# Two of eight token pairs read in a turned layout and normalised there, with nine warming products instead of fifteen

## The chip, the cores and the metric

The kernel runs on one core of a Trainium2 chip. The metric is the device time of one execution in microseconds. The engines are TensorE (PE, the matrix engine, with its weight loads shown as PEld), VectorE (DVE), ScalarE (ACT), GpSimd (POOL) and SyncE (SP, which here issues nearly all DMAs). All data are float32.

## What is computed

```python
def reference(x, wqkv, w_phi, wo, w1, b1, w2):      # x: 2048 x 512
    xn = layernorm(x)                                # no scale, no shift, eps 1e-5
    q, k, v = heads(xn @ wqkv)                       # 32 heads of 16
    phi = lambda p: concat(softmax(p), softmax(-p))
    phi_q, phi_k = phi(q @ w_phi), phi(k @ w_phi)    # w_phi: 16 x 16 for each head
    kv, z = phi_k.T @ v, phi_k.sum(tokens)           # over all 2048 tokens
    s = (phi_q @ kv / (phi_q @ z + 1e-6)) @ wo
    g = silu(mish(xn @ w1 + b1) @ w2)                # 512 -> 1792 -> 512
    return x + s * g
```

## The kernel before

The 2048 tokens are 16 tiles of 128, and two neighbouring tiles form a pair c (0 to 7; tiles 2c and 2c+1). Every matrix operand is kept as a high part (rounded to the matrix engine's fp32r format) and a low part, the rest, and each product is made of three: low by high, high by low, high by high. On top of that the products go by a scheme of Strassen's kind with seven products of blocks in place of eight. Each pair needs for it seven blocks of its normalised, turned x, `xc[c][0]` to `xc[c][6]`: three are x's own quarters, four are sums and differences of them (`xs`). For pairs 0 to 3 these blocks are parts of the tiles `fh`, `fl` (seven of each), which the feed-forward part reads directly; for pairs 4 to 7 they lie in one tile `xc<c>`, and two DMAs copy them to a buffer `xd` in memory, from which later parts load them back.

`norm(t)` makes a tile: load x, statistics on DVE (`st`, `mv`), `rs` = 1/sqrt(var + eps) with a power on POOL, `nb` = -mean times rs, the normalisation of `x` on DVE or ACT, then four PE transposes (128x128 each, a product with the identity `ident`) into the PSUM bank `pt<t>`, from which ACT and DVE read the high and low parts and the differences. Ahead of everything PE multiplies a tile of ones with itself into `wake`, 15 times. `phit`, the 128x512 block matrix of w_phi, is `phic` (a DMA) times a mask; `fold` multiplies it into the weights of k and q on PE (`wkf`, `wqf`), so k and q come out with w_phi applied. `ws1` to `ws4` are sums of weight blocks for the seven products.

The order is written out by hand. ORDER lists the parts of the program (N4 is the normalisation of tile 4, Kc0 a product of pair 0 for k and v, Fa0 one of the first feed-forward matrix, P its weights' preparation, G the second feed-forward matrix, E the end). PLAN lists every recorded operation, as part.number, with a letter where an operation can go to more than one engine (V DVE, G POOL, A ACT); the instructions are issued in that order, so it is the order on each engine's queue. PLACE lists the buffer that each new tile takes. The first DMA of PLAN goes to ACT's queue, all others to SP's. Where a POOL operation stands within 24 places behind a DVE operation that shares a port with it, it waits for that one. Line 293 of the profile is the one line from which every recorded operation is issued (294 in the kernel after the change), so that operations are told apart by the names of their tiles: `kx`, `ky`, `kz`, `kj` products for k and v, `qx` to `qz` for q, `fx`, `fy`, `fz` for the first feed-forward matrix, `y` for the second, `kvp` the sum over tokens, `pn`, `pw` the attention's output; `k<t>p`, `k<t>m`, `k<t>e`, `k<t>s`, `k<t>r` the softmax of tile t; `ha`, `hb`, `hc` the feed-forward sums; `w1a`, `w1s` its weights, each with h and l for the two parts.

Of the kernel before, what the change touches and what calls it, by code (L numbers as in the profile page):

```python
# [16 lines left out]
P = 128  # L17
# [11 lines left out]
WAKE, EACH, NEAR = 15, 2, 24  # L29
# [12 lines left out]
N4.0 N1.0 @.0 @.15 @.1 N4.3 @.2 @.17 @.3 N0.0 @.4 wv0.0 @.5 @.18 @.6 @.7 N4.1 @.19 @.8 @.9 N1.1 wv1.0 @.10 @.16G @.11  # L42
@.20 @.12 N4.2 N1.2 @.13 wq1.0 N1.3 @.14 N4.4 N1.4 N2.0 kh.0 N4.5 N1.5 N4.6 N1.6V N0.1 N4.7 N1.7 kh.1 N4.8 N5.0 N0.2
N1.8 N4.9V wv0.1 N2.3 N6.0 N0.3 kh.2 N0.4 N4.10 N8.3 P4.0 kh.4 N0.5 N4.11 N0.6V N5.1A N6.3 N1.9 wv0.2G N0.7 N4.12 kh.5
kh.3 N5.2 kl.0 N0.8 kh.6 kh.7 wv1.1 N4.13 wq0.0 kl.4 N1.10 wv1.2G N0.9 kl.1 Ka2.0 N1.11 kd.0 N12.0 kl.2 N4.14 N8.0
N0.10 wq1.1 kl.3 N1.12A b1.0 P0.0 Ka2.1A N0.11 kd.1G Ka2.2 N5.3 N2.1 wq1.2A N5.4 N2.2 N2.4 kl.5 N5.5A Ka0.0 N1.13 N2.5
N1.14 N2.6 Ka2.3 N2.7 Ka0.1 N5.6 N1.15G N3.0 kl.6 N5.7 N3.1A N5.8G N1.16 Kc0.0 kl.7 N1.17 Ka0.2A N2.8 N1.18G N8.4
N2.9A wq1.3 k4.0G N1.19 N6.1 N6.4 N2.10 wq1.4A N3.2 N2.11 Kc0.1 N1.20 N2.12 N10.0 N3.3 N2.13 N1.21V k2.0 N3.4 ks.0G
wq0.1 N1.22 N8.1 N3.5A Kd0.0 N2.14 N5.9 wq0.2A Kc0.2A N5.10 N6.2 N3.6 wq0.3 N3.7 ks.1 Kd0.1 N6.5 k2.1V N3.8V N8.2 N8.5
wq0.4A N6.6 N8.6 P0.5 N3.9 wq1.5 N12.3 wq0.5 Kb0.0 Kc0.3 N8.7 N6.7 N3.10 Kd0.2A Kc0.4 N3.11G k4.1 Kb0.1 N5.11G N3.12  # L50
N9.0 N7.0 Kd0.3 N9.1A P0.6G Ka1.0 N8.8 Kc0.5V N5.12 N3.13 N7.1A Kc0.6V Kb2.0 N3.14G ks.2G P0.1G Kd0.4 Kd0.5V Kb0.2V
N6.8 N8.9A Ka1.1A Ka1.2 Kc0.7 N5.13 Kd0.6V N8.10 Kb1.0 N3.15 Ka1.3 N6.9A P0.2G Kc0.8 N5.14G N8.11 N8.12 Kd0.7 k4.2G
Kb1.2 N6.10 N1.23 Kb1.1V Kc0.9 N6.11 N9.2 N7.2 N7.3 N5.15 N5.16 N3.16 Kd0.8 Kc1.0 N9.3 Kb2.1A P0.3G N1.24G N6.12 Kb2.2
# [266 lines left out]
def block_kernel(ctx: ExitStack, tc: tile.TileContext, x, wqkT, wv, phi, wo, w1, b1, w2, out):  # L320
# [33 lines left out]
    def f32(t):  # L354
        return t.bitcast(F32)
# [43 lines left out]
    for _ in range(WAKE):  # L399
        PE.matmul(wake, ones, ones, start=True, stop=True)  # L400
# [704 lines left out]
```

## Time and profile before

| | |
|---|---|
| median of 3 runs | 485.85 us (485.78 to 486.92) |
| the profiled execution | 485.87 us |
| its span, first to last instruction | 484.2 us |
| PE busy | 478.1 us, 99% |
| DVE, ACT, POOL busy | 444.5, 286.7, 262.7 us |
| granted PE clock | full in all slices |

The span is what the rows of the profile cover; 1.7 us of the execution lie around it. Busy shares are averages: PE's matmuls overlap, each row's duration includes its pipeline, and the chain of waits shows what a group of them moves the end by. In rows of groups the columns are line, engine, operation, out<-in with the number of rows, then busy us and mean ns. A row of the waits names who waits, for whom, and the us in total, the number of times and the longest.

### The profile page before, as it was taken

To read this page: it belongs to the slowest core of one execution; us is meant where nothing else is said; L and a number is where in the kernel's file an instruction comes from. 1 tells how busy PE (TensorE), PEld (TensorE's weight loads), DVE (VectorE), ACT (ScalarE), POOL (GpSimd) and SP (SyncE) were. 2 spreads that over 40 slices of the span, in tenths; PEclk is the share of its full clock that TensorE was granted. 3 is DMA by queue.
4 is the path that set the end of the run, shared out by engine and by line. 5 is a ranking of instruction groups with operands and counts; after the bars stand their busy time and mean duration, and the time that the engine had idled before them with its cause. 6 is when DMAs were issued, how large, how long until landed. Compare 5 with 4: busy or idle time off the path is not lost.

```text
span 484.2 us, 10225 instructions
## 1 busy us (share of the span) xinstructions
PE 478.1 (99%) x3820; PEld 426.1 (88%) x3820; DVE 444.5 (92%) x874; ACT 286.7 (59%) x450; POOL 262.7 (54%) x219
## 2 busy tenths in 40 slices
PE   8999999999999999999999999999999999999996
PEld 7888888888888899889888778788999999999996
DVE  6999999899999989999999999989897899999985
ACT  4896645656446343453425745576868677699711
POOL 4988988885671275897888575350312231120042
PEclk9999999999999999999999999999999999999999
DMA  8921672779876889977875739633766346747354
GB/s 309 324 88 45 204 243 63 265 228 303 346 265 211 310 333 375 322 223 247 259 280 153 293 115 345 213 106 126 242 219 206 96 138 203 229 134 214 121 192 145
DMA packets 68642, 105.70 MB, mean 218 GB/s; under 512 B 6896, under 2 KB 37744, under 8 KB 68592
## 3 DMA queue, kind: packets, MB, share of 16 engines
q1 hardware_dynamic: 68448, 104.79, 64.5%
q8 instruction: 30, 0.49, 0.4%
q10 hardware_dynamic: 144, 0.26, 0.2%
q14 instruction: 20, 0.16, 0.1%
HBM read 60.60 MB, written 44.43 MB: 217 GB/s over the span
## 4 chain that ended last, share of the span: by engine, by line
PE 97%; DVE 1%; DMA 1%; POOL 0%; ACT 0%; issue 0%
PE y L293 29%; PE fx L293 16%; PE pw L293 9%; PE fy L293 8%; PE kx L293 8%; PE qx L293 5%; PE ky L293 4%; PE fz L293 4%; PE qy L293 2%; PE kj L293 2%; PE pn L293 2%; PE kz L293 2%; PE kvp L293 2%; PE pt L293 1%; PE qz L293 1%; PE wqf L293 1%
## 5 line engine op out<-in xcount | busy, mean ns | idle before, releaser
L293 POOL TENSOR_TENSOR r<-r 128x128 f32<-128x128 f32 (+1 forms) x40 | 24.5, 626 | 90.8 <-DVE al L293 30.5
L293 DVE TENSOR_TENSOR al<-r,ah 128x896 fp32r<-128x896 f32 x55 | 59.3, 1094 | 8.0 <-PE y L293 3.5
L293 ACT ACTIVATE ah<-r 128x896 fp32r<-128x896 f32 x56 | 52.4, 947 | 21.2 <-PE y L293 7.7
L293 PE MATMUL y<-w2h,al 128*128 128x256 f32 x160 | 45.4, 284 | 0.0
L293 PE MATMUL y<-w2h,ah 128*128 128x256 f32 x160 | 45.3, 283 | 0.0
L293 PE MATMUL y<-w2l,ah 128*128 128x256 f32 x160 | 45.3, 283 | 0.0
L293 PE MATMUL y<-w2t,ah 128*128 128x256 f32 x224 | 42.3, 283 | 0.0
L293 DVE TENSOR_TENSOR r<-r 128x128 f32<-128x128 f32 (+1 forms) x128 | 39.6, 354 | 1.3 <-POOL r L293 1.2
L293 ACT ACTIVATE r<-r 128x512 f32<-128x512 f32 x56 | 33.1, 621 | 10.3 <-DMA r<-hd 10.2
L293 PE MATMUL fx<-fh,w1b 128*128 128x512 f32 x112 | 38.5, 391 | 0.0
L293 PEld LDWEIGHTS y<-w2t,ah 128*128 128x128 f32 x224 | 34.9, 192 | 0.0
L293 PE MATMUL y<-w2t,al 128*128 128x256 f32 x112 | 31.7, 283 | 0.0
L293 PE MATMUL y<-w2g,ah 128*128 128x256 f32 x160 | 31.6, 283 | 0.0
L293 PEld LDWEIGHTS y<-w2h,al 128*128 128x128 f32 x160 | 30.7, 192 | 0.4 <-ACT w2m L293 0.4
L293 PEld LDWEIGHTS y<-w2l,ah 128*128 128x128 f32 x160 | 30.7, 192 | 0.0
L293 PEld LDWEIGHTS y<-w2h,ah 128*128 128x128 f32 x160 | 30.7, 192 | 0.0
L293 PEld LDWEIGHTS fx<-fh,w1b 128*128 128x128 f32 x112 | 21.1, 188 | 4.6 <-issue 0.4
L293 PEld LDWEIGHTS y<-w2g,ah 128*128 128x128 f32 x160 | 24.9, 192 | 0.1
L293 PE MATMUL y<-w2g,al 128*128 128x256 f32 x80 | 22.6, 283 | 0.0
L293 PE MATMUL fx<-fl,w1b 128*128 128x512 f32 x56 | 21.9, 391 | 0.0
L293 PEld LDWEIGHTS y<-w2t,al 128*128 128x128 f32 x112 | 21.5, 192 | 0.0
L293 POOL TENSOR_TENSOR sr<-yy,sr 128x512 f32<-128x512 f32 x3 | 3.8, 1293 | 29.3 <-DVE al L293 25.9
(769 smaller groups left out, 1719.4 us busy)
## 6 DMA issues: line engine op xcount, KB each, us to landing
r<-hd SPq DMA_DIRECT2D x56, 256.0 KB, 3.6
xd<-xc SPq DMA_DIRECT2D x8, 896.0 KB, 5.7
w1b<-w1d SPq DMA_DIRECT2D x14, 512.0 KB, 5.6
w1b<-w1d SPq DMA_DIRECT2D x14, 384.0 KB, 5.8
so<-so SPq DMA_DIRECT2D x16, 256.0 KB, 3.4
x<-x SPq DMA_DIRECT2D x15, 256.0 KB, 4.8
w1a<-w SPq DMA_DIRECT2D x7, 512.0 KB, 4.5
w1d<-w1sh SPq DMA_DIRECT2D x7, 512.0 KB, 2.9
```

Of the source, the lines that this page charges most:

```text
L293: ins = getattr(e, m)(*a, **k)
```

## The change

- A new array xT holds pairs 6 and 7 of x turned ahead of time: for each pair four 128x256 blocks, 512 KB in all, with the features on the partitions and the tokens along the row. Tiles 12 to 15 are made by the new `turned(c)`. x itself is still loaded, token by row, for the statistics, which ACT makes with accumulating passes; mean and factor are turned by a small DMA to memory (`md`) and spread over the partitions by another (`mb`); `xt`, the load of xT, is then shifted and scaled along its rows by two 128x1024 operations. The blocks are split and subtracted from `xt` in SBUF; there are no transposes, no `pt`, no `nb` and no `xr` for these tiles.
- WAKE is 9 instead of 15, and the warming products are one entry of PLAN.
- PLAN and PLACE are new as a whole; ORDER is as it was. `phic` is the first DMA (on ACT's queue), and `phit` is made on DVE; it was POOL's.

```diff
-WAKE, EACH, NEAR = 15, 2, 24
+TURNED = (6, 7)
+WAKE, EACH, NEAR = 9, 2, 24
...
-N4.0 N1.0 @.0 @.15 @.1 N4.3 @.2 @.17 @.3 N0.0 @.4 wv0.0 @.5 @.18 @.6 @.7 N4.1 @.19 @.8 @.9 N1.1 wv1.0 @.10 @.16G @.11
+@.1 @.0 N4.3 @.2V N4.4 N4.0 @.5 kl.0 N1.0 N4.1 @.3 N4.2 N0.0 wv0.0 @.4 wq1.0 N4.5 wv1.0 N4.6 N4.7 N1.1 N5.0 N4.8 N1.2
...
     wake = bank([P, P], "wake")
-    for _ in range(WAKE):
-        PE.matmul(wake, ones, ones, start=True, stop=True)
+    with one():
+        for _ in range(WAKE):
+            PE.matmul(wake, ones, ones, start=True, stop=True)
...
+    def turned(c):
+        mv = alloc("st", [P, 2, 2], f"mv{c}")
+        for i in range(2):
+            xx, junk = load_x(2 * c + i), s2(f"junk{c}{i}")
+            A.activation(junk, xx, AF.Copy, scale=-1.0 / D, accum_out=mv[:, i, 0:1])
+            A.activation(junk, xx, AF.Square, bias=mv[:, i, 0:1], accum_out=mv[:, i, 1:2])
+        V.tensor_scalar(mv[:, :, 1], mv[:, :, 1], 1.0 / D, 1e-5, op0=ALU.mult, op1=ALU.add)
+        G.tensor_tensor(mv[:, :, 1], mv[:, :, 1], mhalf, op=ALU.pow)
+        md = dram.tile([4, P], F32, name=f"md{c}")
+        Q.dma_start(md.rearrange("a p -> p a"), mv.rearrange("p t m -> p (t m)"))
+        mb = s2(f"mb{c}")
+        Q.dma_start(mb, md.rearrange("a p -> (a p)")[None, :].to_broadcast([P, D]))
+        xt, d = slot([P, 4, 2, P], f"xt{c}"), slot([P, 4, 2, P], f"xs{c}")
+        Q.dma_start(xt.rearrange("p b k n -> p (b k n)"), xT[TURNED.index(c)].rearrange("p b k n -> p (b k n)"))
+        u = xt.rearrange("p (t b) k n -> p t (b k) n", t=2)
+        m = mb.rearrange("p (t m n) -> p t m n", t=2, m=2)
+        for i, op in ((0, ALU.add), (1, ALU.mult)):
+            either(u, u, m[:, :, i, None, :].to_broadcast([P, 2, 4, P]), op=op)
...
+            w = alloc("tq", [P, 2, 7, 2, P], f"xc{c}", F32R)
...
+            xc[c] = [(w[:, 0, x], w[:, 1, x]) for x in range(7)]
+            split(xt[:, 0:3], w[:, 0, 0:3], w[:, 1, 0:3], either)
+        for i, a, b in ((0, xt[:, 3], xt[:, 0]), (1, xt[:, 2], d[:, 0]), (2, xt[:, 2], xt[:, 3]), (3, xt[:, 1], d[:, 1])):
+            either(d[:, i], a, b, op=ALU.subtract)
...
+        split(d, w[:, 0, 3:], w[:, 1, 3:], either)
+        for u in range(2):
+            Q.dma_start(xd[:, u, :, :, c % 4, :].rearrange("p c k n -> p (c k) n"), f32(w)[:, u].rearrange("p c k n -> p (c k) n"))
+
     def norm(t):
+        if t // 2 in TURNED:
+            if t % 2 == 0:
+                turned(t // 2)
+            return
```

The start of PE's queue before, up to the first block product:

```order
L293 MATMUL wake_99<-ones_84 128x128 x15
L293 MATMUL wkf01_147<-phit_101,wkT00_137 128x128 x4
L293 MATMUL pt1_173<-ident_83,x1_170 128x128 x4
L293 MATMUL pt4_156<-ident_83,x4_151 128x128 x4
L293 MATMUL wkf11_148<-phit_101,wkT01_138 128x128 x4
L293 MATMUL pt0_167<-ident_83,x0_164 128x128 x4
L293 MATMUL pt5_184<-ident_83,x5_153 128x128 x4
L293 MATMUL wkf21_181<-phit_101,wkT10_139 128x128 x4
L293 MATMUL wkf31_182<-phit_101,wkT11_140 128x128 x4
L293 MATMUL kx2_187<-wv0h_142,fl00_104 128x512
```

The same place after the change:

```order
L294 MATMUL wake_99<-ones_84 128x128 x9
L294 MATMUL wkf21_181<-phit_101,wkT10_139 128x128 x4
L294 MATMUL wkf01_147<-phit_101,wkT00_137 128x128 x4
L294 MATMUL pt4_156<-ident_83,x4_151 128x128 x4
L294 MATMUL pt5_184<-ident_83,x5_153 128x128 x4
L294 MATMUL pt1_173<-ident_83,x1_170 128x128 x4
L294 MATMUL wkf11_148<-phit_101,wkT01_138 128x128 x4
L294 MATMUL pt0_167<-ident_83,x0_164 128x128 x4
L294 MATMUL wqf21_192<-phit_101,wqT10_190 128x128 x4
L294 MATMUL wqf31_193<-phit_101,wqT10_190 128x128 x4
L294 MATMUL kx2_187<-wv0h_142,fl00_104 128x512
```

A second fold has moved ahead of the first transposes, tile 1 behind tiles 4 and 5, and two folds of q have taken the place of one of k.

DVE at the start before (behind its three constants); `st` and `mv` are a tile's statistics:

```order
L293 BN_STATS st4_152<-x4_151 128x6
L293 BN_STATS st1_171<-x1_170 128x6
L293 BN_AGGR mv4_150<-st4_152 128x2
L293 BN_AGGR mv1_169<-st1_171 128x2
L293 TENSOR_SCALAR rs1_168<-mv1_169 128x1
L293 BN_STATS st5_154<-x5_153 128x6
L293 BN_AGGR mv4_150<-st5_154 128x2
L293 TENSOR_SCALAR nb1_172<-mv1_169,rs1_168 128x1
L293 TENSOR_SCALAR rs4_149<-mv4_150 128x2
L293 TENSOR_SCALAR x1_170<-x1_170,mv1_169,rs1_168 128x512
```

The same place after:

```order
L294 TENSOR_TENSOR phit_101<-phic_100,bmask_88 128x512
L294 BN_STATS st5_154<-x5_153 128x6
L294 BN_STATS st4_152<-x4_151 128x6
L294 BN_AGGR mv4_150<-st4_152 128x2
L294 BN_AGGR mv4_150<-st5_154 128x2
L294 TENSOR_SCALAR rs4_149<-mv4_150 128x2
L294 BN_STATS st1_171<-x1_170 128x6
L294 TENSOR_SCALAR nb5_183<-mv4_150,rs4_149 128x1
L294 TENSOR_SCALAR nb4_155<-mv4_150,rs4_149 128x1
L294 BN_AGGR mv1_169<-st1_171 128x2
L294 TENSOR_SCALAR x5_153<-x5_153,mv4_150,rs4_149 128x512
```

`phit` now stands ahead of all statistics on DVE, and tiles 5 and 4 share one `rs` ahead of tile 1.

DVE where pair 7 is made, before; `hc` is the add that both orders have there:

```order
L293 TENSOR_TENSOR xc7_393<-pt14_392,xc7_393 128x512
L293 TENSOR_TENSOR hc4_396<-hc4_396,fx4_381 128x512
L293 TENSOR_REDUCE k10m_402<-k10p_399 128x32
L293 TENSOR_TENSOR xc7_393<-pt15_405,xc7_393 128x256
L293 TENSOR_TENSOR hb4_395<-hb4_395,fy4_394 128x512
L293 TENSOR_TENSOR ha4_383<-ha4_383,fz4_382 128x512
L293 TENSOR_REDUCE k9s_357<-k9e_359 128x64
L293 TENSOR_TENSOR k8e_369<-kx4_311,k8m_368 128x32x16
L293 TENSOR_TENSOR xs7_406<-xr7_407,pt14_392 128x256
```

And after:

```order
L294 TENSOR_TENSOR hc4_394<-hc4_394,fx4_378 128x512
...
L294 TENSOR_TENSOR ha4_380<-ha4_380,fz4_379 128x512
L294 TENSOR_REDUCE k10m_400<-k10p_397 128x32
L294 TENSOR_TENSOR xs7_390<-xt7_389 128x256
L294 TENSOR_TENSOR xc7_391<-xt7_389,xc7_391 128x768
L294 TENSOR_TENSOR xs7_390<-xt7_389,xs7_390 128x256
L294 TENSOR_TENSOR xs6_352<-xt6_351,xs6_352 128x256
L294 TENSOR_TENSOR xs7_390<-xt7_389 128x256
L294 TENSOR_TENSOR k9e_360<-k9p_355,k9m_359 128x32x16
L294 TENSOR_TENSOR xs7_390<-xt7_389,xs7_390 128x256
L294 TENSOR_TENSOR xc6_353<-xs6_352,xc6_353 128x1024
L294 TENSOR_TENSOR xc7_391<-xs7_390,xc7_391 128x1024
```

The blocks now come from `xt` in SBUF, in two large splits for each pair, and stand closer together; between `hc` and `ha` two more reductions of the softmax stand where the dots are.

More of the change, by code (lines that the diff above doesn't have):

```diff
@@ new lines @@
+N1.8 N4.11 b1.0 N6.3 P0.0 N12.0 N0.3 kh.2 N0.4 N0.5 kh.4 N0.6V kh.3 N4.12 kl.2 N0.7 kh.5 kh.6 N1.9 wv0.2G kh.7 wq1.1
+wq1.3 N4.13 N5.3 N5.4 N0.8 N0.9 wq1.2A wv1.1 N5.5A wq1.4A N0.10 N1.10 kd.0 N4.14 kl.3 N5.6 N1.11 N0.11 N14.0 wq1.5
+wv1.2G Ka2.0 kl.4 Ka0.0 N1.12V N1.13 N2.1 kl.5 Ka2.1A Ka0.1 N1.14 kd.1G kl.6 N2.2 N2.4 Ka0.2A N5.7 N2.5 N1.15V N2.6
+kl.7 Ka2.2 Kc0.0 wq0.1 N1.16 N2.7 Kc0.1 N5.8G N3.0 N5.9 N2.8 N6.1 Ka2.3 N1.17 N1.18G N3.1A N2.9A N5.10 wq0.2A N2.10
+N3.2 k4.0G N1.19 N1.20 N8.4 N8.1 N6.2 N6.4 N1.21G N5.11G N2.11 Kc0.2A k4.1 Kd0.0 N3.3 N1.22 N2.12 N5.12 N8.2 N2.13
@@ new lines @@
+P0.5 k2.0 ks.0G Kd0.1 N3.4 N8.5 N3.5V N6.5 N2.14 wq0.3 N5.13 wq0.4A Kb0.0 Kc0.3 N3.6 N3.7 Kd0.2A ks.1 N6.6 N8.6 k2.1V
+N3.8V N3.9 Kb0.1 N3.10 Kb0.2A N1.23 Kc0.4 N6.7 N8.7 N9.0 N6.8 N6.9A N7.0 Ka1.0 Kc0.5V Ka1.1V N8.8 N3.11G Kc0.6V N3.12
+P0.1G Kb2.0 ks.2G N5.14G Kd0.3 Kd0.4 N9.1A N7.1A N3.13 Kb2.1A Kd0.5V N3.14G N3.15 N8.9A Kb1.0 Kb1.1A Kc0.7 N1.24G
+k4.2G P0.2G Ka1.2 Ka1.3 Kd0.6V Kd0.7 N5.15 Kc0.8 N8.10 Kb1.2 N7.2 N6.10 N9.2 Kb2.2 N5.16 N8.11 N6.11 N7.3 N9.3 Kd0.8
+Kc2.0 Kc1.0 Kb2.3A Kc2.10 N6.12 N9.4 N8.12 N3.16 N9.5A N6.13 N7.4 N7.5A Kb1.3A N12.1 N9.6 N6.14 N9.7 Kc1.1 P0.6G
@@ new lines @@
+Kd4.0 Kd4.1A Kd3.6 N12.11G P4.6V Kb5.0 Kb5.2 Kb5.1A Kb5.3A Kc5.0 Fa4.2 Fa4.0 Kd3.7 Kc3.9G Kd3.8 Kd3.9V Kc5.1 A3.2
+P4.3G N12.12V P4.4V A2.1V P4.7 Fa4.1A Kc5.10 Kd5.0 P4.8V Fb4.0 N12.13 Kd5.1A Fb4.1A P4.10 N14.10 P4.11 P4.12 A3.0G
+Ka5.3 Fb4.2 Kc5.11 Kd4.2 Kc4.3 Fb4.3A N12.14V N12.15V N14.11V Fc4.0 Kc4.11 Fc4.1 Kd4.3 Kc5.2 Fa4.3 N14.12G N12.16G
+N12.17G Fc4.3 Fd4.0 P3.0 P6.0 P1.0 Kd5.2 N14.13 N14.15V N14.14V N14.16V N12.18V N14.17V Ka6.0 Fd4.1A Ka6.1A N12.19
+Ka6.2 Kc4.4V N14.18V N14.19 N12.20V Ka7.2 Ka7.0 Fa4.4 N12.21 P2.0 Fc4.2 wQ.0 N14.20V P3.5 Ka7.1A P6.5 P6.9 P5.0 Kb6.0
@@ new lines @@
+D13.6 R0.6G D11.10 D14.4 G7.2V D15.4 R2.0 O1.2 R3.0 Fd7.2 D14.5 D13.7 D14.6 D15.5 D13.8V D14.7 D12.9 D15.6 H2.5 G11.0
+D13.9 D12.10 R5.0 D14.8G D15.7 D14.9 G7.3G D15.8V G7.4V D15.9 G8.2G R1.2G Ua1.0 D13.10 G7.5 O7.1A R0.8V R0.10V O7.2
+D14.10 R1.3G Fc7.5 G11.1 G10.1 G11.2V G7.6V G9.1 Ua1.1 R1.5 Ua1.2 R1.4G O2.1V Ua1.3 G1.2G G8.3G G11.3G Ua1.4 O4.1V
+G10.2G R1.9 Ua1.5 Ua1.6 R1.7 Ua1.9 O6.0 O6.1A Ua1.7 G8.4G R1.10G O6.2 D15.10 Ua1.10 Ua1.8 R1.8G Ua1.13 Ua1.11 G8.5
+Ua1.14 Ua1.12 R1.6V G8.6V R2.1G R4.1G R2.2G O5.2 O2.2 G13.0 G3.0 R4.2G G1.3G G10.3G G30.2G O3.2 Fd13.2 G7.12 G7.9
@@ new lines @@
+G13.2V O11.0 O11.1A R5.8V R2.6V G13.3V R2.8V G9.6V G28.6V R4.4V O14.2 G0.0 R3.7 O13.1A O8.0 O13.2 G2.0 G31.0 G4.0
+G12.4V R3.10V O15.1V R3.8G G29.5 G29.6V G10.6V R3.6V O8.1A G0.1 G12.5 G11.5 R4.7 R4.9 G4.1 R4.5 G9.9 G9.12 G28.7
+G28.12 G9.7 G28.9 G28.10 G28.8 G28.11 G28.13 O11.2 G5.0 G33.0 G11.6V G9.13 G9.8 G9.10 R4.8V G3.3V G12.6V G13.4V R4.6V
+G13.5 G30.4V G13.6V G4.2V G10.9 G10.7 G10.12 R4.10G G29.12 G10.13 G10.10 G9.11 G29.11 G6.0 G17.0 G29.7 G29.13 G10.8
+G33.1 G30.5 G29.9 G11.12 G11.9 G31.1 G10.11 G29.10 G34.0 O9.2 G11.13 G11.10 G11.7 G30.6V G29.8 G11.11 G12.11 G14.0
@@ new lines @@
+G26.1 G39.5 G22.5 G21.4V G24.1 G38.6V G40.3V G42.3V G39.6V G40.4V G27.2V G24.2V G26.2V G37.11 G37.8 G37.13 G20.10
+G20.8 G38.7 G37.10 G40.5 G42.4V G40.6V G38.12 G38.9 G38.10 G38.11 G39.9 G38.8 G38.13 E2.0A G21.5 G47.1 G39.12 G43.0
+H4.4 H2.6 G45.0 G39.7 G39.11 G39.10 G39.13 G40.12 G39.8 G40.11 G24.3G E2.1 G26.3V G25.4V G22.6V E2.2 G43.1 G23.5 G41.5
+G47.2G G27.3G G40.7 E2.3 G49.44V G21.6V G49.45G G24.4G E2.4 E2.5 H2.1 G40.9 G40.13 G40.10 G40.8 G21.9 G21.12 G21.10
+G21.13 G22.9 G21.11 G21.7 G44.0 G41.6V E2.6 G42.5 G23.6V G43.2V G48.0 H5.5 G49.14 H2.7V G43.3V H2.8V H2.2V G43.4V
@@ L170 @@
+E7.10 E7.17 E7.27 E7.28 E7.29 E7.30
 """
@@ L319, in block_kernel @@
 @with_exitstack
-def block_kernel(ctx: ExitStack, tc: tile.TileContext, x, wqkT, wv, phi, wo, w1, b1, w2, out):
+def block_kernel(ctx: ExitStack, tc: tile.TileContext, x, xT, wqkT, wv, phi, wo, w1, b1, w2, out):
     nc = tc.nc
@@ L473, in stats @@
         G.tensor_tensor(rs, rs, mhalf[:, 0:n], op=ALU.pow)
+    def turned(c):
[16 more added lines that the diff above has]
+            either(u, u, m[:, :, i, None, :].to_broadcast([P, 2, 4, P]), op=op)
+        if c < 4:
+            xc[c] = [tuple(u[:, :, c * P:(c + 1) * P] for u in ts) for ts in fx[0]]
+            for i in range(3):
+                split(xt[:, i], *xc[c][i], either)
+        else:
+            w = alloc("tq", [P, 2, 7, 2, P], f"xc{c}", F32R)
+            prog.region[w.tensor.name] = 14 * 2 * P, lambda e: (e // (14 * P), (0, 0, 0, 2, 2, 2, 2)[e // (2 * P) % 7])
+            xc[c] = [(w[:, 0, x], w[:, 1, x]) for x in range(7)]
+            split(xt[:, 0:3], w[:, 0, 0:3], w[:, 1, 0:3], either)
+        for i, a, b in ((0, xt[:, 3], xt[:, 0]), (1, xt[:, 2], d[:, 0]), (2, xt[:, 2], xt[:, 3]), (3, xt[:, 1], d[:, 1])):
+            either(d[:, i], a, b, op=ALU.subtract)
+            if c < 4:
+                split(d[:, i], *xc[c][3 + i], either)
+        if c < 4:
+            return
+        split(d, w[:, 0, 3:], w[:, 1, 3:], either)
+        for u in range(2):
+            Q.dma_start(xd[:, u, :, :, c % 4, :].rearrange("p c k n -> p (c k) n"), f32(w)[:, u].rearrange("p c k n -> p (c k) n"))
@@ L1086 @@
     w1b = [w1[:, :, k, f] for k, f in ((0, 0), (1, 0), (1, 1), (0, 1))]
+    xT = np.asarray(A_x)[0].reshape(NT // 2, 2, P, 2, 2, P).transpose(0, 5, 1, 3, 4, 2)[list(TURNED)]
     arrays = {
         "x": np.ascontiguousarray(np.asarray(A_x)[0]),
+        "xT": np.ascontiguousarray(np.stack([xT[:, :, 0, 0], xT[:, :, 0, 1], xT[:, :, 1, 1], xT[:, :, 1, 0]], 2)),
         "wqkT": np.ascontiguousarray(wqkv[:, :2 * D].reshape(KC, P, 2, KC, P).transpose(2, 0, 4, 3, 1).reshape(2 * KC, P, KC, P)),
```

228 lines of the change are left out of this document (99 added, 129 removed), and 44 rows, old and new, of the table PLACE.

## Prediction

> **What bounds the kernel now.** I began with the first lines of the page and its chain, then the waits of the matrix engine.
>
> ```profile
> span 484.2 us, 10225 instructions
> ...
> PE 478.1 (99%) x3820; PEld 426.1 (88%) x3820; DVE 444.5 (92%) x874; ACT 286.7 (59%) x450; POOL 262.7 (54%) x219
> ...
> PE 97%; DVE 1%; DMA 1%; POOL 0%; ACT 0%; issue 0%
> ```
> ```profile
> PE wake L293 <- DVE mhalf L394: 1.1, 1, 1.1
> PE pt L293 <- DVE rs L293: 1.0, 1, 1.0
> ```
>
> PE is busy for 99% of the span, the chain is 97% PE, and PE waits twice in all, both times before the first block product. So a microsecond of PE work taken out is a microsecond gained, as long as the other engines keep delivering in time; work taken off DVE, ACT or POOL by itself gains nothing. What isn't PE lies at the two ends. The chain of waits, its end first, then its start:
>
> ```profile
> 464.98 15.25 PE y L293 x127
> ...
> 480.25 0.39 ACT u L293
> ...
> 480.67 0.44 DVE u L293
> ...
> 481.13 0.42 DVE xx L293
> ```
> ```profile
> 0.80 3.48 DMA x<-x
> ...
> 4.30 1.29 DVE st L293 x2
> 5.59 0.23 DVE mv L293 x2
> ...
> 5.84 0.15 DVE rs L293
> ...
> 7.54 0.71 POOL rs L293
> ...
> 8.28 0.34 DVE nb L293 x2
> ...
> 9.21 0.64 PE pt L293 x4
> 9.84 0.89 PE wkf L293 x8
> ```
>
> From 9.21 to 480.23 us the chain is PE without a break, 471.0 us. Ahead of that stands the arrival of x4, its statistics and its normalisation; behind it some 4 us of last adds and a store. The change keeps the order of parts, and the tail's last operations are the same, so I give the tail nothing.
>
> **The transposes that go.** Here are the row of all transposes, and the chain where four of those of the last four tiles stand:
>
> ```profile
> L293 PE MATMUL pt<-ident,x x64: 270/272/328, 7.5 to 97.9; 128*128 128x128 f32 x64
> ```
> ```profile
> 82.75 0.44 PE pt L293 x4
> 83.19 1.39 PE kx L293 x6
> ...
> 86.41 1.36 PE ky L293 x6
> ```
>
> The 270 ns is the length of one matmul with its pipeline; the chain shows that four of them move the end by 0.44, or 0.11 each. Sixteen of the 64 go: 4 x 0.44 = 1.75 us off PE. The group behind a transpose takes 1.39 and not 1.36, so a switch of shape costs 0.03. Counted over the whole order, there are 2 fewer switches between 256 and 512 columns and 4 fewer from 128x128 to 512: 6 x 0.03 = 0.17. The other products are the same in number and kind. Middle of the kernel: -1.9 us, if nothing takes it back.
>
> **The warming products and the start.** PE's rows, and windows of its warming products alone (length, PE busy and passes, weight loads, granted clock):
>
> ```profile
> 1.12 5.68 PE L293 MATMUL wake<-ones 128*128 128x128 f32 x30 [1.12 <-DVE mhalf L394]
> 6.63 1.06 PE L293 MATMUL wkf<-phit,wkT 128*128 128x128 f32 x8
> ```
> ```profile
> 1.12:3.12 2.00, 2.00 (x9) 2.00 (x10) 1.00 0.61 156
> ...
> 5.60:6.40 0.80, 0.80 (x9) 0.80 (x9) 1.00 1.03 366
> ```
>
> 15 products are 30 passes. Nine in the first window take 2.00 us, 0.22 each; from 5.6 nine take 0.80, under half of that. With 9 products the 18 passes end at about 1.12 + 18 x 0.213 (0.22 less the edges) = 5.0 us instead of 6.6. That alone gives nothing, because PE then waits for phit and x4; what counts is how much useful work is done before the point from which PE never waits again. Before: at 9.21 it had done one fold (0.89) and one transposed tile (0.44), so 9.21 - 1.33 = 7.88 us were lost.
>
> After: phic goes first on ACT's DMA queue and phit, its product with the mask, is DVE's; x5 and x4 are first on SP's. The prices:
>
> ```profile
> x<-x ACTq DMA_DIRECT2D x1, 256.0 KB, 3.5
> ...
> phic<-phi SPq DMA_DIRECT2D x1, 32.0 KB, 3.2
> b1t<-b SPq DMA_DIRECT2D x1, 7.0 KB, 8.0
> ```
> ```profile
> 10.16 0.81 ACT L293 ACTIVATE x<-x,nb,rs 128x512 f32<-128x512 f32 x1
> 11.11 0.68 DVE L293 TENSOR_TENSOR ws<-wvr,wkf 128x512 f32<-128x512 f32 x1
> ```
>
> phic lands at 0.8 + 3.2 = 4.0 or somewhat sooner, phit takes 0.68 on DVE (the row of ws, same shape), so the statistics of x5 and x4 start at s = 4.3, where x4 stood before; between 4.0 (phit quicker) and 4.8 (phic late). Then two statistics 1.29, two mv 0.23, rs 0.15, POOL's pow 0.71, two nb 0.34, ACT's normalisation of x4 0.81 and 0.15 between them: the transposes of x4 at s + 3.7 = 8.0. While the pow runs DVE does the statistics of x1 and then mv, x5, rs, POOL's second pow (one column, so at most the 0.71 of two, beside DVE's st0), nb and x1: pt1 at s + 4.9 = 9.2, by the same rows. Another rs, pow, nb and normalisation of x0 put pt0 at s + 6.2 = 10.5. Until then PE has two folds, three transposed tiles and one more fold to do: 3 x 0.89 + 3 x 0.44 = 3.99. The folds in front end long before 8.0, pt1 and the third fold fill 9.2 to 10.5 exactly, and from pt0 on the rows of PE have their data. Lost: 10.55 - 3.99 = 6.56 us. Gain 7.88 - 6.56 = 1.3; with s between 4.0 and 4.8, 1.6 to 0.8. I take 1.2, a little under the middle, because wkT01 and wqT10 (sixth and seventh among the big transfers) have under half a microsecond to spare.
>
> The Trainium skill, "TensorE: Matmul & The Clock Gate", section "Part 1: The HAM clock gate", says that a cold TensorE runs at half rate until it has been kept busy for a window of about 3.4 us; the halving of the pass time at about 5.5 us agrees, though the clock column reads 1.00 on both sides of it. By that rule 9 products, which stop at 5.0, may not have warmed it; what that would cost is worked out from rows as part of the first rival.
>
> **The turned pairs beside PE.** Pairs 6 and 7 lose the statistics, normalisations and reads out of PSUM of four tiles, and get two passes of ACT for each tile, two small DMAs (md turns 128x4 numbers into rows in memory, mb spreads them over 128 partitions), a load of 512 KB, and two 128x1024 operations on POOL and DVE. The busy sums stay within 3 us per engine by like rows, with DVE at the same sum. Off PE's path that costs nothing, unless a block arrives late. The DMA chain has slack: by the place of its pow in POOL's order md7 is issued between 72 and 78 us, and even at 8.0 us for each of the two (b1t, the longest small DMA above) mb7 is there by 94, with its first use on DVE at about 96. The same skill's "DMA: Bandwidth & Descriptors", section "Rules for kernel authors", makes a transfer with a strided last dimension one descriptor per element, and md is 512 of them; the row nearest to that is b1t's, and the slack covers it.
>
> The narrow place is DVE just before the products of the two pairs. Its rows, and PE's beside them:
>
> ```profile
> 99.40 0.69 DVE L293 TENSOR_TENSOR xc<-pt,xc 128x512 fp32r<-128x512 f32 x1
> 100.00 0.68 DVE L293 TENSOR_TENSOR hc<-hc,fx 128x512 f32<-128x512 f32 x1
> ...
> 106.87 0.42 DVE L293 TENSOR_TENSOR xs<-pt,xr 128x256 f32<-128x256 f32 x1
> 107.20 0.42 DVE L293 TENSOR_TENSOR xs<-pt,xs 128x256 f32<-128x256 f32 x1
> ```
> ```profile
> L293 DVE TENSOR_TENSOR w1sl<-w1s,w1sh 128x1024 fp32r<-128x1024 f32 x5 | 6.2, 1243 | 0.0
> ...
> L293 DVE TENSOR_TENSOR w1al<-w1a,w1ah 128x768 fp32r<-128x768 f32 x2 | 1.9, 950 | 0.0
> ```
> ```profile
> 104.47 1.36 PE kx L293 x6
> 105.83 2.72 PE kz L293 x12
> 108.55 2.72 PE kx L293 x12
> ```
>
> Ahead of the first kx of pair 6 stand 342 block products in both orders, so this point moves by the two terms above, from 104.47 to about 101.3; kz7 follows at 104.1, the summed kx6 at 106.8 and kx7 at 108.1. The add hc on DVE waits for the fx product that ends two groups (2.7 us) before 101.3, so it starts at 98.6 at the earliest. From there, at the pitch of the rows (0.60 for 512 elements, 0.33 for 256, 0.9 for 768, 1.15 for 1024): four more 512s to 101.6, one 256 to 101.9, the lows of xc7 (768) done at 102.9, needed at 104.1; three 256s, a 512 and a 256 to 104.8, the lows of xc6 at 106.0, needed at 106.8; those of xc7 at 107.2, needed at 108.1. Margins 1.2, 0.8 and 0.9 us. Behind hc there is another: the fx product at 100.0 writes the bank that hc reads until 99.3, 0.7 us. All hold, so this costs 0, and each microsecond by which DVE is later than I make it, past about 0.7, costs one.
>
> **Sum.** 485.87 for the profiled execution (its span 484.2 and 1.7 around it; the median of the three runs is 485.85, the same) - 1.75 - 0.17 - 1.2 = 482.75, so 482.8 us, 0.6% faster. About 0.3%, 1.46 us, is what a measurement of this kernel can tell from no change: faster is below 484.4, slower above 487.3.
>
> **Rivals.** First, the start gains nothing: phic or x5 comes late, or PE is cold again. In the latter case passes at 0.21 instead of 0.107 until about 8.9 us hit little but the folds and pt4, and delay pt0 by about 0.65: 483.4; with the whole term lost 484.0. For it speaks that the rate doubled only at 5.5, after the time at which the shorter warming ends; against it that folds follow at once.
>
> Second, DVE is late in the first 30 us, where its list is re-dealt: the summed wv lows are due at 31.6 by PE's order and done at 29.5 by the sum of its rows; before there were 5 us there. 0 to 2 us lost: 483 to 485.
>
> Third, and on the other side: the turned blocks of pairs 6 and 7 come late at kz7, kx6 or kx7. This window shows how full DVE is:
>
> ```profile
> 100.00:110.00 10.00, 10.00 (x165) 8.24 (x164) 9.36 (x18) 5.96 (x8) 9.56 (x8) 1.00 0.64 204
> ```
>
> DVE works 9.36 of 10 us and POOL 9.56, so a delay has nowhere to be made up. The price is the delay less the margin of 0.7: the gain of 3.1 is eaten when DVE (or the POOL multiply and the ACT round in front of it) is 3.8 us late, and the kernel is slower by 0.3% from 5.2 us, 487.5. For it: nothing of this chain has run before in this place, and 128x1024 with a broadcast operand has no row. Against it: the sums above, and that PE never waited in this stretch.
>
> **Chances.** Forecast, 482.0 to 483.8: 0.58. Start without gain: 0.14 (0.05 for the slow passes at 483.4, 0.09 for the whole term at 484.0), of which 0.02 within 0.3% where some of the other terms fails too. DVE late early, 483 to 485: 0.08, half of it faster. Turned blocks late: 0.20, of which 0.08 within 0.3% and 0.12 beyond. Faster 0.58 + 0.12 + 0.04 = 0.74; same 0.02 + 0.04 + 0.08 = 0.14; slower 0.12. The range runs from 481.9 (s at 4.0 and a margin for the counted switches) to 485.4 (the second rival whole and the beginning of the third), which leaves out most of the third rival, some 0.16, and little below.
>
> **What would show it.** Right: PE waits only before 10.6 us, the first wkf by 5.1, the x4 transposes at 8.0; kx of pair 6 near 101.3; 48 rows of pt; the last y ends near 477.1. Wrong: a wait of PE kx, kz or fx on DVE at 100 to 109 us, on ws at 31, or wkf passes at 0.21 after 5 us. The step most likely to be wrong is the 0.7 us margin of DVE.

## The result and the profile after

The changed kernel takes 489.71 us (median of five runs, 488.1 to 491.3) against 486.3 of the kernel before: a ratio of 1.0072 (95% interval 1.0044 to 1.0099). It is slower by 0.7%, where 0.6% faster was forecast; 489.7 lies above the range. The profiled execution took 490.39 us. One execution of 954.3 us in the last experiment below and one of 523.2 us of the kernel before beside it lie far from all others and are left out of every number. The head of the changed kernel's page and the waits of PE:

```profile
span 488.7 us, 10155 instructions
...
PE 477.6 (98%) x3792; PEld 422.7 (86%) x3792; DVE 448.1 (92%) x857; ACT 285.3 (58%) x456; POOL 268.9 (55%) x226
```
```profile
PE pt L294 <- ACT x L294: 1.4, 1, 1.4
PE wkf L294 <- DMA wkT<-wqkT: 1.2, 1, 1.2
PE wake L294 <- DVE mhalf L395: 1.1, 1, 1.1
PE fx L294 <- ACT xc L294: 1.0, 1, 1.0
PE pn L294 <- issue: 1.0, 1, 1.0
PE kx L294 <- ACT v L294: 0.8, 1, 0.8
PE kx L294 <- POOL xc L294: 0.2, 1, 0.2
PE fx L294 <- DVE hc L294: 0.2, 1, 0.2
```

Before, PE waited twice, and only ahead of the first product. Now it also waits at four places between 85 and 106 us and once at 321 us. Three starts split the difference (the chain before had pair 6's first kx at 104.47, its last y ended at 480.23). The start before and after, then pair 6 and the end after:

```profile
13.22 0.48 PE L293 MATMUL kx<-wv0h,fl 128*128 128x512 f32 x1
```
```profile
10.23 1.53 PE L294 MATMUL pt<-ident,x 128*128 128x128 f32 x12 [1.38 <-ACT x L294]
...
14.89 0.50 PE L294 MATMUL kx<-wv0h,fl 128*128 128x512 f32 x1
```
```profile
107.20 1.36 PE kx L294 x6
```
```profile
484.59 0.39 ACT u L294
```

- Start: the first block product begins at 14.89, before at 13.22, with one fold of 0.89 more done by then: 0.8 us lost, where 1.2 gained was forecast.
- Up to kx of pair 6: 107.20 - 104.47 = 2.7 later, of which 0.8 is the start, and 1.75 us of transposes are gone: 2.7 - 0.8 + 1.75 = 3.7 us lost on the way. The rows of the four new waits add up to 2.2 of it; no row names the rest, but all 3.7 go together with the waits (the turn on DVE, below).
- From there to the end: 484.57 - 107.20 = 377.4 against 375.8: 1.6 more, about the stall in pn and what stands round it.

0.8 - 1.75 + 3.7 + 1.6 = 4.35, the difference of the two ends of PE's work.

Timelines of the changed kernel show where these waits come from, with SP's queue first (start, length of the issue, transfer), then POOL, DVE and ACT:

```profile
77.83 0.37 SPq L294 DMA_DIRECT2D md<-mv  x1
78.24 1.43 SPq L294 DMA_DIRECT2D xt<-xT  x1
87.72 0.32 SPq L294 DMA_DIRECT2D mb<-md  x1
```
```profile
89.74 2.41 POOL L294 TENSOR_TENSOR xt<-xt,mb 128x1024 f32<-128x1024 f32 x1 [4.25 <-issue]
92.11 2.92 POOL L294 TENSOR_TENSOR k7e<-k7e,k7r 128x1024 f32<-128x1024 f32 x1
```
```profile
90.72 2.50 DVE L294 TENSOR_TENSOR k6e<-k6e,k6r 128x1024 f32<-128x1024 f32 x1
...
93.75 2.36 DVE L294 TENSOR_TENSOR xt<-xt,mb 128x1024 f32<-128x1024 f32 x1
96.74 0.43 DVE L294 TENSOR_TENSOR w1s<-w1a,w1s 128x256 f32<-128x256 f32 x1 [0.63 <-POOL w1s L294]
```
```profile
76.15 0.60 ACT L294 ACTIVATE k9p<-ky 128x512 f32<-128x512 f32 x1 [2.48 <-DMA hd<-ha]
...
97.20 1.06 ACT L294 ACTIVATE w1sh<-w1s 128x1024 fp32r<-128x1024 f32 x1 [7.37 <-DVE w1s L294]
```

md is issued at 77.83 and mb, which waits for its data, only at 87.72: 512 single numbers, 2 KB, take nearly 10 us. xt6, issued right behind md at 78.24, lands at 89.7, 11.4 us later, and POOL's add starts with it. So that add and then k7e run at the same time as two operations of DVE of the same size, and these take 2.50 and 2.36 us; 128x1024 operations of DVE took 1.2 before. POOL's part of w1s, behind k7e on its list, is then late, DVE waits 0.63 us for it at 96.74, ACT's w1sh and DVE's w1sl follow, and PE's fx waits 1.0 us until 99.67.

This can't be behind the two waits of PE that end at 85.5 and 89.4, ahead of it. Earlier on SP's queue a transfer of hd stands behind mb6, which waits for md6 until 70.80; ACT's k9p idles 2.5 us for that hd, and what follows on ACT and DVE starts late. Transfers issued ahead of md7 are late as well: w1ah (73.09) and two of hd (75.73 and 76.29) land after 12.9, 11.5 and 11.1 us, where no w1ah and no hd between 57 and 70 us took over 4.0 in the kernel before.

### The profile page after: what moved, and what is told of

Same layout as the page of the kernel before. It is cut to its first block, busy times and chain, and to the rows that moved or that the text cites. A ratio compares the mean times of both kernels' runs of the same rounds, so it can differ in the third digit from the quotient of the medians.

```text
span 488.7 us, 10155 instructions
## 1 busy us (share of the span) xinstructions
PE 477.6 (98%) x3792; PEld 422.7 (86%) x3792; DVE 448.1 (92%) x857; ACT 285.3 (58%) x456; POOL 268.9 (55%) x226
## 4 chain that ended last, share of the span: by engine, by line
PE 77%; issue 0%; DVE 0%; ACT 0%
PE y L294 29%; PE fx L294 14%; PE pw L294 9%; PE fy L294 7%; PE qx L294 5%; PE fz L294 3%; PE qy L294 2%; PE pn L294 2%; PE kx L294 2%; PE qz L294 1%; PE ky L294 1%; PE kvp L294 1%; PE kz L294 1%; PE pz L294 0%; DVE u L294 0%
## 5 line engine op out<-in xcount | busy, mean ns | idle before, releaser
L294 POOL TENSOR_TENSOR r<-r 128x128 f32<-128x128 f32 (+1 forms) x49 | 30.7, 649 | 63.7 <-DVE r L294 23.1
L294 DVE TENSOR_TENSOR r<-r 128x128 f32<-128x128 f32 (+1 forms) x119 | 37.9, 355 | 4.8 <-ACT r L294 2.5
L294 PE MATMUL fx<-fh,w1b 128*128 128x512 f32 x112 | 37.3, 390 | 0.0
```

The costliest lines, as they stand in the source:

```text
L294: ins = getattr(e, m)(*a, **k)
```

## The experiments

Times are medians. Each ratio compares with the kernel before on the same chip (485.8 to 486.3 us) and has its 95% interval behind it; differences in us between two changed kernels are between medians of different series.

### ACT's table load at once

```diff
     phic DMA on ACT's queue
+    A.activation(warm, mhalf, AF.Identity)      # two columns, read by nobody
```

> The changed kernel with a two-column ACT operation right behind the first DMA on ACT's queue, so that ACT's table load (1.28 us) no longer stands behind the wait for nb of tile 4. If the late table load is what holds the start: the first transposes at about 8.95 us instead of 10.23, tile 0's at about 11.4 instead of 12.50, and the time 1.0 to 1.3 us below the changed kernel's 489.7, near 488.6. If the start is held by the arrival of x1 and wkT10 instead, or if the later waits absorb it: no change at kx of pair 6 (107.2 us) and a time within 0.3 us.

489.55 us, 1.0079 (1.0049 to 1.0110). The start did what the theory said:

```profile
8.64 1.74 PE L294 MATMUL pt<-ident,x 128*128 128x128 f32 x12
...
13.51 0.50 PE L294 MATMUL kx<-wv0h,fl 128*128 128x512 f32 x1
```
```profile
PE ky L294 <- ACT k9p L294: 1.2, 1, 1.2
```

The first transposes are 1.6 us earlier and the first product 1.4, yet the time is the same within the noise: a wait of 1.2 us of ky for ACT's k9p takes the place. So the late table load is a real cost of the start, and in this order something later takes most of what it gives back.

### The spreading DMA later on SP's queue

```diff
-... N12.8 Fc0.2 N12.9 Kc1.7 ...   N14.7 A2.0G N14.8 ...   N11.11G N14.9 ...   P4.10 N14.10
+... N12.8 Fc0.2 Kc1.7 ...   N12.9 N14.7 A2.0G N14.8 ...   N11.11G ...   P4.10 N14.9 N14.10
```

> The changed kernel with the two spreading DMAs mb6 and mb7 later on SP's queue (mb6 just ahead of md7, mb7 just ahead of the load xt7), so that the DMAs behind them no longer stand behind a wait for md. If SP's queue is what is held (theory Q): hd is issued at about 65 us instead of 71.2, ACT's k9p and DVE's 1.5 us of idle at 77 go, and the PE waits at 85 to 106 us (2.0 us) shrink to under 1; time 1.5 to 3 us below 489.7. If DVE's list is simply too long (theory D): the waits stay and the time is within 0.5 us. If xt6's slow landing (11.4 us) is the main part, the wait at 99.7 stays although the DVE idle at 77 goes: 0.5 to 1 us gained.

490.64 us, 1.0093 (1.0078 to 1.0108). It gained nothing. POOL still waited for xt6, until 88.4 us, and a stall of PE of 3.1 us inside the kvp products came up:

```profile
74.80 0.50 PE L296 MATMUL kvp<-k3e,v 128*32 128x64 f32 x18
78.41 0.42 PE L296 MATMUL kvp<-k3e,v 128*32 128x64 f32 x14 [3.11 <-issue]
```

The marks of theory Q did come: hd<-ha was issued at 63.99, and PE's waits between 85 and 106 us are gone. But a PE that stands 3.1 us at 75 also gives DVE and ACT that much time. So the run shows that the move gains nothing, and doesn't decide whether the held queue was behind those waits.

### md without single numbers, values misplaced

```diff
-        md = dram.tile([4, P], F32, name=f"md{c}")
-        Q.dma_start(md.rearrange("a p -> p a"), mv.rearrange("p t m -> p (t m)"))
+        md = dram.tile([P, 4], F32, name=f"md{c}")
+        Q.dma_start(md, mv.rearrange("p t m -> p (t m)"))
```

> The changed kernel with md written without the turn, 16 bytes in a row for each partition, so that means and factors of pairs 6 and 7 stand in other places of mb; all else is as it was. If md's 512 single numbers are the slow part: md lands in 2 to 4 us instead of 8 to 10, mb is issued 5 us earlier, xt6 lands in about 7 us, POOL's add of xt6 starts near 86 instead of 89.7 and no longer runs beside DVE's k6e (2.50 us, 1.21 alone); the waits at 85 to 106 us shrink to under 1 us, time 2 to 4 us below 489.7. Under theory D the time stays within 0.5 us.

485.38 us, 0.9981 (0.9972 to 0.9991): 4.3 below the changed kernel, with the same bytes, the same number of DMAs and the same order of every instruction. The issues of this kernel (KB each, median us to landing), its waits of PE, all of them ahead of 10 us, and DVE's two operations:

```profile
md<-mv SPq DMA_DIRECT2D x2, 2.0 KB, 1.4
```
```profile
PE wkf L294 <- DVE mv L294: 1.4, 1, 1.4
PE pt L294 <- ACT x L294: 1.3, 1, 1.3
PE wake L294 <- DVE mhalf L395: 1.1, 1, 1.1
```
```profile
88.87 1.42 DVE L294 TENSOR_TENSOR k6e<-k6e,k6r 128x1024 f32<-128x1024 f32 x1
...
90.81 1.38 DVE L294 TENSOR_TENSOR xt<-xt,mb 128x1024 f32<-128x1024 f32 x1
```

All four waits between 85 and 106 us are gone.

### Fifteen warming products again

```diff
-WAKE, EACH, NEAR = 9, 2, 24
+WAKE, EACH, NEAR = 15, 2, 24
```

> The changed kernel with 15 warming products again. If the shorter warming leaves the matrix engine slow (theory W), the first folds take 0.9 instead of about 1.0 each and the time falls by 0.2 to 0.6 us. If the start is held by the table load and the arrival of x1: the warming ends at 6.6, the folds at about 8.6, still ahead of the transposes at 10.2, and the time stays within 0.3 us of 489.7.

489.67 us, 1.0073 (1.0058 to 1.0088): no difference. The number of warming products is no part of the result. In both kernels the first transposes wait 1.4 us for ACT's x in any case, so this says nothing about a start that ACT doesn't hold.

### md in rows, mb read with a step

```diff
         (md as in the run with misplaced values)
-        m = mb.rearrange("p (t m n) -> p t m n", t=2, m=2)
+        m = mb.rearrange("p (n t m) -> p t m n", t=2, m=2)
```

> The changed kernel with md written 16 bytes in a row for each partition, and the two 128x1024 operations reading mb with a step of four numbers, so that each mean and factor reaches its token. If md's single numbers are the whole cause and the step costs nothing on DVE and POOL: xt's add on POOL 2.40 us and its multiply 1.2 us alone as before, no PE wait of 0.2 us or more after 11 us, time 485.4 as with the misplaced numbers, that is 4.3 below the changed kernel. If the step slows the two operations (to 2 or 4 times): the waits at kz7 and kx7 come up, 487 to 490.

487.31 us, 1.0025 (1.0016 to 1.0034). Better by 2.4 than the changed kernel, worse by 1.9 than with misplaced values; the step of four numbers costs where mb is read:

```profile
L294 POOL TENSOR_TENSOR xt<-xt,mb x2: 2891/2934/2977, 84.0 to 102.2; 128x1024 f32<-128x1024 f32 x2
L294 DVE TENSOR_TENSOR xt<-xt,mb x2: 1980/2123/2266, 91.5 to 100.0; 128x1024 f32<-128x1024 f32 x2
```

DVE needs 2.0 to 2.3 us in place of 1.2 to 1.4, and fx waits 0.9 us for hc: the narrow place of 0.7 us that the prediction named. Its trace also has a stall of 1.0 us in pn.

### The same with the early table load

> The same with ACT's early table load. If the start's 1.3 us counts as soon as nothing absorbs it later: 484.0, 1.4 below the run with md alone, 2.3 below the kernel before. If DVE between 15 and 110 us is the bound, so that an earlier start meets waits again: PE waits near 76 and 88 us and 485 to 485.4.

487.11 us, 1.0025 (1.0009 to 1.0040): the same as without it. PE's wait for hc stays at 0.9 us. But in this trace the earlier start hardly came about:

```profile
6.05 3.77 PE L294 MATMUL wkf<-phit,wkT 128*128 128x128 f32 x16 [0.73 <-DVE st L294]
...
14.47 0.50 PE L294 MATMUL kx<-wv0h,fl 128*128 128x512 f32 x1
```

The 16 passes of the first two folds took 0.21 us each, the pace of the first warming products, though the clock column reads 1.00; in eight of the ten traces with nine products the same 16 took 2.3 to 2.4 us, a longer wait between the two folds left out. The other slow one is that of the next kernel, xt6 ahead of md7. The first product came at 14.47, only 0.3 ahead of the run without the early load (14.76). So the run doesn't show what an earlier start would meet on DVE; it shows the prediction's first rival, PE slow again.

### xt6 ahead of md7

```diff
-... N14.7 A2.0G N14.8 N12.10 N11.4 ...
+... N14.7 A2.0G N12.10 N14.8 N11.4 ...
```

> The changed kernel with the load xt6 one place ahead of md7 on SP's queue; md is unchanged. If the single numbers of md7 slow the transfer behind them: xt6 lands 4 to 6 us after its issue instead of 11, POOL's add of xt6 no longer runs beside DVE's k6e, the waits at 89 and 99.7 us shrink and the time falls by 1.5 to 3.5 us to 486 to 488. If what hurts is the wait for md itself (mb7 and what stands behind it): xt6 as late or no gain, 489 to 490.

490.32 us, 1.0083 (1.0056 to 1.0110). xt6 now landed in 6.5 us, and k6e took 1.41, so the collision of DVE and POOL was gone; but md itself still took 10.2 (the median of its two), and the load of the next pair became the late one:

```profile
103.10 1.23 DVE L296 TENSOR_TENSOR xt<-xt,mb 128x1024 f32<-128x1024 f32 x1 [2.69 <-DMA xt<-xT]
```

### Two unread DMAs of md's form in the kernel before, and their control

```diff
+    two DMAs on SP's queue, behind N12.7 and N14.7:
+    Q.dma_start(dram.tile([4, P]).rearrange("a p -> p a"), ident[:, 0:4])    # 512 single numbers
     control: dram.tile([P, 4]), 128 rows of 16 bytes
```

> The kernel before with two DMAs of md's form (128x4 numbers turned, 512 single ones) added on SP's queue at the statistics of tiles 12 and 14; nobody reads them or waits for them. If such a transfer only slows its neighbours in the queues: the xd or w1d transfers behind it take 3 to 6 us longer, and with the slack of the kernel before the time moves by 0 to 1 us. If it costs PE time by itself whatever the slack: 488 or more.

> Control for the two unread DMAs added to the kernel before: the same two, at the same places, with 128 rows of 16 bytes in place of 512 single numbers. If the form is what costs: the added DMAs land in 1.5 to 3 us and the time is that of the kernel before, 486.1, within 0.5. If any further DMA at these places costs that much: 490 to 494, as with single numbers.

494.52 us (490.7 to 497.3), 1.0173 (1.0106 to 1.0240), with single numbers, and 486.22 us, 1.0007 (0.9998 to 1.0016), with rows. Nobody reads these 2 KB. Their landing, single numbers first and rows second, DVE's timeline with single numbers, and the landing of x15's load with them and in the kernel before:

```profile
xm<-ident SPq DMA_DIRECT2D x2, 2.0 KB, 12.3
```
```profile
xm<-ident SPq DMA_DIRECT2D x2, 2.0 KB, 3.5
```
```profile
76.86 0.69 DVE L293 BATCH_NORM_STATS2 st<-x 128x6 f32<-128x512 f32 x1 [3.31 <-DMA x<-x]
```
```profile
DMA to landing us min/median/max: 7.6/7.6/7.6
```
```profile
DMA to landing us min/median/max: 2.5/2.5/2.5
```

x15's load, issued at 69.2 us, 0.4 ahead of the first of the two, landed in 7.6 us; in the kernel before it took 2.5. DVE idled 3.3 us for it, and PE 1.5 after it; two stalls inside kvp cost PE another 2.5. The time that such a transfer costs is not the price of its own data. The windows from 72 to 84 us, with single numbers and in the kernel before (last two columns: DMA share, GB/s), show that the 16 DMA engines were not busy with it:

```profile
72.00:84.00 12.00, 10.46 (x54) 8.40 (x50) 8.69 (x17) 6.59 (x12) 8.25 (x7) 1.00 0.02 1
```
```profile
72.00:84.00 12.00, 12.00 (x67) 10.00 (x60) 11.53 (x21) 7.34 (x13) 10.64 (x8) 1.00 0.15 44
```

The Trainium skill, "DMA: Bandwidth & Descriptors", section "Queues, rings and completion order", says that an issuing engine's queue is a ring on each of the same DMA engines, in which descriptors start in order. That what SP issues behind a slow transfer is late agrees with it. It doesn't explain why x15, issued ahead, was late too; how a slow transfer delays its neighbours stays open.

### The turn on DVE

```diff
-        Q.dma_start(md.rearrange("a p -> p a"), mv.rearrange("p t m -> p (t m)"))
+        V.transpose(mz, mw)                       # 128x32, in blocks of 32; mv is mw[:, 0:4]
+        with one():
+            for b in range(4):
+                Q.dma_start(md[:, 32 * b:32 * b + 32], mz[32 * b:32 * b + 4, :])
```

> The changed kernel with the small turn done on DVE (a transpose of 128x32 in blocks of 32) and md written as four DMAs of four rows of 128 bytes; pair 7's md stands behind the load xt6. All values reach their places and mb is read without a step. If the single numbers of md are the cause of all waits after the start: md lands in about 2 us, no PE wait over 0.2 us between 15 and 130 us, time near that of the run with 16-byte rows, 485.4 (485.0 to 486.0). If the four DMAs and the wait of DVE's transpose for POOL cost as much as they save: 487 or more.

485.39 us, 0.9993 (0.9984 to 1.0003): the time that md in rows of 16 bytes gave, with all values in place and without the step in mb. This kernel also issues md7 later, behind xt6; the run with misplaced values kept the order, so the form alone is enough. The waits of PE in this kernel, and its chain at pair 6:

```profile
PE pt L296 <- ACT x L296: 1.3, 1, 1.3
PE wkf L296 <- DVE mv L296: 1.3, 1, 1.3
PE wake L296 <- DVE mhalf L401: 1.1, 1, 1.1
```
```profile
101.83 1.36 PE fx L296 x6
103.19 1.36 PE kx L296 x6
```

kx of pair 6 starts at 103.19, 1.3 ahead of the kernel before. The first product begins at 14.69, 0.6 later than before with one fold more done, so nothing of the 3.7 us is left.

### The turn on DVE and the early table load

> The same with ACT's early table load. If the start's 1.4 us counts when no later wait absorbs it: 484.0 (483.6 to 484.6), 2 us under the kernel before. If DVE's list has no slack behind the start: waits of PE on DVE or ACT between 70 and 110 us and the same time as without the early load.

484.89 us, 0.9974 (0.9962 to 0.9985). This version beats both kernels, the one before by 1.0 us and the changed one by 4.8. The first product stands 1.0 us earlier than without the early load (13.72 against 14.69), and by the medians half of it reaches the end. In the two profiled executions pair 6 is still 0.95 ahead, and a stall inside pn takes most of it:

```profile
312.99 2.70 PE L296 MATMUL pn<-ph,kvw 32*32 32x256 f32 x104
316.37 0.69 PE L296 MATMUL pn<-ph,kvw 32*32 32x256 f32 x24 [0.68 <-issue]
```

### The transposes twice, in the kernel before

```diff
             for k in range(KC):
-                PE.transpose(pt[:, k, :], xx[:, k * P:(k + 1) * P], ident)
+                for _ in range(2 if t >= 12 else 1):
+                    PE.transpose(pt[:, k, :], xx[:, k * P:(k + 1) * P], ident)
```

> The kernel before with each of the 16 transposes of tiles 12 to 15 done twice. If the price of a transpose is what the chain of waits gave, 0.11 us, and PE is the bound there: 1.75 us more, 487.8 (487.6 to 488.1). If the weight loads or the pipeline make a transpose cost its whole row, 0.27: 490.4. If it is hidden by other waits: 486.1.

487.77 us, 1.0036 (1.0024 to 1.0048): 1.85 more than the kernel before (485.92), 0.116 for a transpose.

### Both moves at once, and unread single numbers in the repaired order

```diff
 both moves:   mb6 and mb7 later, xt6 ahead of md7 (the two edits above together)
 unread:       the kernel with the turn on DVE, and two unread DMAs of 512 single numbers,
               one behind mb6, one just ahead of xt6
```

> The changed kernel with both moves at once: mb6 and mb7 later on SP's queue and xt6 one place ahead of md7; md is still written as 512 single numbers. If the two ways, the wait of mb on the queue and the slow xt6 behind md7, are the whole harm: 486 or less, no PE wait over 0.5 us between 70 and 110 us. If the single numbers slow whatever is in flight beside them, so that other transfers become late instead: 488.5 to 491, with a PE wait of 1 us or more at another place.

> The kernel with the turn on DVE (485.4) and two unread DMAs of 512 single numbers added, one behind mb6 and one just ahead of xt6; nobody waits for their data. If slowing its neighbours is what such a transfer does: xt6 lands in 9 to 12 us again and the time is 488 to 491. If only the wait for md's own data does harm: 485.4 to 486.

491.05 us, 1.0106 (1.0088 to 1.0124), for both moves: k9p of ACT still waited 1.5 us for an hd transfer, one that SP had issued 1.8 us behind md6 and that landed over 10 us later, and PE stalled 2.6 us inside kvp. 489.92 us, 1.0093 (1.0059 to 1.0126), for the unread ones; no trace shows where this kernel's time goes. 485.4 became 489.9 by two transfers that nobody waits for. So the loss comes back whole without anyone waiting for the data of a single-number transfer: its price is what it does to the transfers beside it.

## Why the prediction was wrong, point by point

- **The transposes: right.** 16 of them were put at 1.75 us by the chain of waits; done twice they cost 1.85, and from the first product to pair 6 PE is shorter by as much in the three traces without a wait there (misplaced values, and the turn on DVE with and without the early load).
- **"The DMA chain has slack": the step that failed.** Its sum held: 8.0 us was taken for md and for mb, md took 7.9 and 9.8 and mb 4.6 and 4.3, and mb7 was there at 92, inside the 94 allowed. But the step priced md only by who waits for it. The transfers next to it on SP's queue, xt6 above all, whose loads the prediction didn't walk at all, pay for it as well, and the prediction had put that at nothing. With md in rows and the same order 4.3 us of the 6.9 by which the median missed are gone; with two unread transfers of the old form in the repaired kernel 4.5 come back. No rival had this; the third, turned blocks late, named the engine that came late, DVE, but for another cause, and the waits came at 85 to 106 us on products of k and v ahead of pair 6's and on fx, not at kz7, kx6 or kx7.
- **DVE's list at the two pairs: right once its data came in time.** With the turn on DVE there is no wait of PE on it at 100 to 109 us. The 0.7 us behind hc was the narrowest place, as said: 0.8 to 0.9 us more in each of DVE's two operations with a step in their operand brought a wait of 0.9 us there.
- **The start: mis-sized by 2.0 us.** Forecast was 1.2 gained, measured 0.8 lost. The walk had ACT's normalisation of x4 right behind nb. In truth ACT's table load stood between them, and x1's statistics ahead of nb. The table load before and after, ACT's x4, and DVE's x1:

```profile
1.23 1.28 ACT L293 ACT_TABLE_LOAD   x1 [1.23 <-PEq L1097]
```
```profile
8.06 1.28 ACT L294 ACT_TABLE_LOAD   x1 [8.06 <-DVE nb L294]
9.36 0.81 ACT L294 ACTIVATE x<-x,nb,rs 128x512 f32<-128x512 f32 x1
```
```profile
7.06 0.69 DVE L294 BATCH_NORM_STATS2 st<-x 128x6 f32<-128x512 f32 x1 [0.82 <-DMA x<-x]
```

  In the kernel before ACT's first operation waits for PE alone, and its table load runs ahead of that wait; now the first one waits for a DMA, DVE and POOL, and in the order of ACT's queue the load stands behind two of these waits. The early load alone puts the first product 1.4 us forward. The other 0.6 fit x1: DVE idles 0.8 us for its load, and nb stands behind its statistics; no run tests this part alone. The first fold, due by 5.1, began at 6.53, when its weights had landed; that cost nothing, since the transposes wait for ACT until 10.23.
- **"Tail: nothing": nearly.** The last adds are as before; but a stall in pn at 321 us, 1.0 us by the waits, is new. It stands inside a run of products that by the order wait for nothing, and is there in three of the traces (0.7 to 1.0 us). kvp has the like in three others, all with single numbers in flight: 3.1 and 2.6 us in the two kernels with mb later, 1.2 and 1.3 in the kernel before with unread single numbers. The packets in the traces point at PE's own instructions. pn stops after 104 of its 128 products in all three traces, kvp after 18 of its last 32 in both kernels with mb later. In these five traces PE goes on some 1.4 us after one 16 KB packet of the queue that the page lists as "q8 instruction" has ended: 318.9 to 320.5 in the changed kernel, where PE goes on at 321.85, and 76.1 to 77.0 with mb later, where it goes on at 78.41. With mb later that packet starts at 76; in the kernels without a stall there one starts at 65 to 71. Beside the unread single numbers a packet of this queue that starts at 72.4 takes 4.0 us, beside the control's rows 2.4 (from 72.8), in the kernel before 1.4. So single numbers seem to delay this queue as well, and PE with it. No run tests that, and why pn stops, with no single numbers near, stays open.
- **The clock rival: not what happened here, but not out for every start.** Fifteen warming products instead of nine change nothing in the changed kernel. In two of the ten traces with nine products, though, the first folds ran at 0.21 us a pass, and in the one with md in rows and the early load that took the start's gain.

In sum: forecast 482.75; the start +2.0, the loss ahead of pair 6 +3.7, pn and what is round it +1.6, and 0.2 of shape switches that didn't show: 490.3, against 490.39 of the profiled execution.

## What to carry to other kernels

A small DMA that turns numbers (one number per piece) has two prices: the time to its data, and what it does to the transfers beside it. Price the second by walking the transfers issued shortly ahead of it and behind it, even where nobody waits for the small one; a transpose of 32x32 blocks on DVE and rows of 128 bytes bought the same turn for nothing measurable. And when the first operation of an engine changes, look at what is loaded ahead of it, and behind which waits.

## What the runs showed that was not expected

- 512 single numbers, 2 KB, take 8 to 12 us to land, and a 256 KB load issued 0.4 us ahead takes 7.6 us in place of 2.5. As 128 rows of 16 bytes the same 2 KB take 1.4 to 3.8 us, and two of them unread move the time by no more than the noise.
- DVE's 128x1024 operation takes 2.4 to 2.5 us in place of 1.2 when a POOL operation runs beside it. The Trainium skill, "SBUF — State Buffer", section "Terms", says that the two share a pair of ports which one holds for a whole instruction, so that the other is blocked; 2.50 is 1.21 plus most of the rest of POOL's 2.41, which agrees.
- With a step of 16 bytes in its broadcast operand, a 128x1024 operation takes 2.0 to 2.3 us on DVE and 2.9 to 3.0 on POOL (1.2 to 1.4 and 2.4 without).
- Taking off two of the ways by which a slow transfer hurts, one at a time and together, gave back nothing; other waits, or a stall of PE inside kvp, took their place each time.
